# Attention by pairs of heads: the last rows of two heads in one tile, x^T of both in one accumulation, reciprocals spread by TensorE, and an order that a list scheduler makes

## The chip, the cores and the metric

The kernel runs on one core of one Trainium2 chip. Its time is device microseconds of one execution, as the median of several runs; smaller is better. A core has TensorE (PE: matmuls and the weight loads, PEld, that go with them), VectorE (DVE), ScalarE (ACT), GpSimd (POOL) and SyncE (SP), which here issues the DMAs. Each works through its own instructions in order.

## The reference

Three layers follow one another; the change touches the first alone.

```python
# q, k, v: 2 batches x 8 heads x 576 rows x 64;  f: 2 x 8 x 576
scores = scale * (q @ k.T)                      # 576 x 576 a head
cum = cumsum(log(clip(f, 1e-4, 1)))
scores = where(causal, -1e9, scores + cum[:, None] - cum[None, :])
scores -= scores.max(-1)
attn = exp(scores); attn /= attn.sum(-1) + 1e-9
x = attn @ v                                    # -> 1152 tokens x 512
# layer 2: 8 experts on all tokens, each token's expert weights found by 8 rounds of
#          normalising over experts and tokens:  out += P[:, e] * (relu(x @ w1[e]) @ w2[e])
# layer 3: the same with noisy logits, top 2 experts a token
```

All of it is float32. Matrix products are made of float32r parts: a number is split in a high part and the rest (hi, lo), and hi*hi + hi*lo + lo*hi are summed in PSUM.

## The kernel before

Attention comes first, then the gate and layer 2, then layer 3. `attention()` works head by head, 16 heads, two of them (a pair) sharing the 128 rows of x^T. A head's 576 rows are five tiles of rows t = 0..4: four of 128 rows, where tile t needs the first 128 (t + 1) columns, and a last one of 64 rows and 576 columns. The steps of a head, with their lines:

- `split_q` (L237): q is split in hi and lo, stacked as 128 columns; k is loaded twice side by side. `prep_mm` (L288) turns both by TensorE into PSUM (five transposes each), `prep_hi` (ACT) and `prep_lo` (DVE) write q1, k1 and k2 to SBUF.
- `score_mm` (L254): two matmuls a tile and one with the mask. `score_max` (L278, DVE): adds the running sum `cb`, writes P and the row's extreme. `score_exp` (L284, ACT): the exponential and the row's sum.
- `recip` and `weigh` (L319 to L332, DVE): one over the row sums, in two parts a head, and P times it, tile by tile.
- `turn_mm` (L334), `turn_hi` (ACT), `turn_lo` (DVE): P^T by transposes on TensorE, split into `pth` and `ptl`.
- `value_mm` (L360): x^T of the head. The stationary operand holds [v_hi v_lo] in its 128 columns, so that the two halves of the result's rows have to be added: `value_copy` (L374, ACT) brings one half over, `value_add` (L379, DVE) adds it. `x_parts` splits x^T into xh and xl.

PSUM has eight banks: two single ones named t, two named s, two named o, and one double one named w, through which q's and k's transposes and the scores of the last rows go.

The order is written out by hand. Each step has a time in units of a score tile (five a head): `at(g - 5 + t + D_MAX[t], score_max, n, t)`, with the tables D_* at the top; all steps are sorted by that time and issued, each to its engine. In the second batch's heads (from g = 50) the 96 matmuls of layer 2's first unit are put between them (`fill_mm`, L396, here called fills: they need xh and xl of the first batch, and expert 0's w1). SP loads q, k, v of a pair and `cb`, a row of the running sum spread over 128 partitions, two pairs ahead.

## Time and profile before

| | |
|---|---|
| three runs | 1254.22, 1255.77, 1260.47 us; median 1255.77 |
| the profiled execution | 1257.79 us, its span 1256.1 us |
| attention, first score to the first matmul behind it | 11.98 to 183.70 us |
| TensorE busy over the span | 1206.5 us (96%), mean granted clock 0.981 |
| DVE, ACT, POOL busy | 575.2, 402.8, 178.0 us |

The page cuts the span into 40 slices of 31.4 us; attention is the first six. A window's row gives the length, then each engine's busy time with its number of instructions, the TensorE clock granted (1.00 is 2.4 GHz, 0.50 is 1.2 GHz), and the DMA engines' share. Matmuls overlap in the records, so TensorE's price of something is read from start to start, not from the duration.

### The profile page before, as it was taken

The page shows a single profiled execution, that of the slowest core. Times are in us where ns is not written, and L with a number is a line of the kernel's source. Part 1 is how long each engine was busy: PE and PEld are TensorE (multiplying, and loading weights), DVE is VectorE, ACT ScalarE, POOL GpSimd, SP SyncE. Part 2 cuts the span into 40 slices and gives each one's busy share as a digit, 9 for nine tenths or more (in the row PEclk, how much of TensorE's full clock was granted, in tenths as well). Part 3 has the DMA queues.
Part 4 walks back from the last instruction along what each step waited for, and adds up shares of the span by engine and source line. Part 5 has one row for each costly group of instructions (what it writes and reads, how often), then busy time and mean ns, then how long its engine had stood idle before and what let it go on. Part 6 is the DMA issues. An engine that isn't in the chain of part 4 may idle for free. (4 is left out here: it accounts for less than half of the span.)

```text
span 1256.1 us, 17681 instructions
## 1 busy us (share of the span) xinstructions
PE 1206.5 (96%) x6965; PEld 1089.3 (87%) x6965; DVE 575.2 (46%) x1203; ACT 402.8 (32%) x796; POOL 178.0 (14%) x276
## 2 busy tenths in 40 slices
PE   7889999999999999999999999999999987999996
PEld 5667789999999999999999999999888877999995
DVE  6999876423323323223233132333455653655541
ACT  5767652212212212112122122122123443444440
POOL 4353320000000000000000000000022124343332
PEclk9988899999999999999999999999999998999998
DMA  6535113202202102012021020222021466686632
GB/s 140 133 97 125 48 52 128 68 1 67 67 2 67 39 29 68 19 49 67 1 68 38 30 68 1 67 68 67 26 93 59 135 198 178 200 224 223 180 103 62
DMA packets 112476, 105.35 MB, mean 84 GB/s; under 512 B 53102, under 2 KB 88046, under 8 KB 112383
## 3 DMA queue, kind: packets, MB, share of 16 engines
q1 hardware_dynamic: 99231, 89.86, 24.3%
q0 software_dynamic: 13152, 14.27, 4.2%
q8 instruction: 56, 0.92, 0.3%
q14 instruction: 37, 0.30, 0.1%
HBM read 94.47 MB, written 9.98 MB: 83 GB/s over the span
## 5 line engine op out<-in xcount | busy, mean ns | idle before, releaser
L131 PE MATMUL h<-xh,w1h 128*128 128x384 f32 (+8 forms) x1056 | 336.7, 319 | 2.8 <-DVE htl L516 2.3
L133 PE MATMUL h<-xh,w1l 128*128 128x384 f32 (+8 forms) x1056 | 334.2, 317 | 0.0
L132 PE MATMUL h<-xl,w1h 128*128 128x384 f32 (+8 forms) x1056 | 334.2, 316 | 0.0
L515 ACT ACTIVATE hth<-h 128x384 fp32r<-128x384 f32 (+8 forms) x264 | 119.0, 453 | 474.6 <-PE h L133 473.5
L521 PE MATMUL y<-w2h,hth 128*128 128x512 f32 (+1 forms) x624 | 244.6, 392 | 0.0
L523 PE MATMUL y<-w2h,htl 128*128 128x512 f32 (+1 forms) x624 | 243.8, 391 | 0.0
L522 PE MATMUL y<-w2l,hth 128*128 128x512 f32 (+1 forms) x624 | 243.6, 390 | 0.0
L516 DVE SCALAR_TENSOR_TENSOR htl<-h,hth 128x384 fp32r<-128x384 f32 (+8 forms) x264 | 132.8, 508 | 185.5 <-ACT hth L515 184.5
L131 PEld LDWEIGHTS h<-xh,w1h 128*128 128x128 f32 x1056 | 199.3, 189 | 5.5 <-DVE htl L516 3.3
L132 PEld LDWEIGHTS h<-xl,w1h 128*128 128x128 f32 x1056 | 199.3, 189 | 1.0
L133 PEld LDWEIGHTS h<-xh,w1l 128*128 128x128 f32 x1056 | 199.3, 189 | 0.0
L523 PEld LDWEIGHTS y<-w2h,htl 128*128 128x128 f32 (+1 forms) x624 | 116.9, 187 | 25.2 <-DVE htl L949 0.2
L522 PEld LDWEIGHTS y<-w2l,hth 128*128 128x128 f32 (+1 forms) x624 | 117.1, 188 | 23.7
L521 PEld LDWEIGHTS y<-w2h,hth 128*128 128x128 f32 (+1 forms) x624 | 117.1, 188 | 23.7
L667 DVE SCALAR_TENSOR_TENSOR acc<-y,Pgate,acc 128x512 f32<-128x512 f32 x52 | 39.0, 750 | 201.7 <-PE y L523 201.7
L849 POOL DMA_INDIRECT table_scratch<-rows,place x18 | 17.5, 975 | 786.7 <-DVE place L841 723.8
L127 DVE TENSOR_TENSOR w1l<-raw,w1h 128x1024 fp32r<-128x1024 f32 x68 | 83.1, 1223 | 75.7 <-ACT w1h L126 73.2
L126 ACT CAST w2h<-raw 128x1024 fp32r<-128x1024 f32 x68 | 70.2, 1053 | 95.6 <-PE y L523 90.8
L127 DVE TENSOR_TENSOR w2l<-raw,w2h 128x1024 fp32r<-128x1024 f32 x68 | 81.0, 1221 | 39.9 <-ACT w2h L126 37.9
L126 ACT CAST w1h<-raw 128x1024 fp32r<-128x1024 f32 x68 | 71.4, 1050 | 82.3 <-PE h L132 54.6
L969 PE MATMUL y<-htl,w2h 128*128 128x282 f32 (+5 forms) x192 | 58.3, 303 | 0.7 <-DVE htl L516 0.7
L967 PE MATMUL y<-hth,w2h 128*128 128x282 f32 (+5 forms) x192 | 58.7, 306 | 0.0
(242 smaller groups left out, 1267.4 us busy)
## 6 DMA issues: line engine op xcount, KB each, us to landing
raw<-in_moe_w_dram SPq DMA_DIRECT2D x136, 512.0 KB
cb<-ncum_scratch SPq DMA_DIRECT2D x7, 576.0 KB
raw_k<-in_k_dram SPq DMA_DIRECT2D x30, 128.0 KB
out_dram<-zer SPq DMA_DIRECT2D x1, 2304.0 KB
x_scratch<-acc SPq DMA_DIRECT2D x9, 256.0 KB
raw_q<-in_q_dram SPq DMA_DIRECT2D x16, 128.0 KB
raw_v<-in_v_dram SPq DMA_DIRECT2D x16, 128.0 KB
raw_k<-in_k_dram SPq DMA_DIRECT2D x15, 32.0 KB
```

The source lines that it names most:

```text
L126: nc.scalar.copy(hv, rv)
L127: nc.vector.tensor_tensor(lv, rv, hv.bitcast(F32), op=OP.subtract)
L131: nc.tensor.matmul(pt[:, :n], w1h[:, kc, fs], ah[:, kc, :], start=kc == 0, stop=False)
L132: nc.tensor.matmul(pt[:, :n], w1h[:, kc, fs], al[:, kc, :], start=False, stop=False)
L133: nc.tensor.matmul(pt[:, :n], w1l[:, kc, fs], ah[:, kc, :], start=False, stop=kc == KC - 1)
L515: nc.scalar.activation(hh[:, fc, :n], pt[:, :n], AF.Relu)
L516: nc.vector.scalar_tensor_tensor(hl[:, fc, :n], pt[:, :n], 0.0, hh[:, fc, :n].bitcast(F32), op0=OP.max, op1=OP.subtract)
L521: nc.tensor.matmul(py[:m], hh[:, fc, ts], w2h[:, fc, :], start=fc == 0, stop=False)
L522: nc.tensor.matmul(py[:m], hh[:, fc, ts], w2l[:, fc, :], start=False, stop=False)
L523: nc.tensor.matmul(py[:m], hl[:, fc, ts], w2h[:, fc, :], start=False, stop=fc == FC - 1)
L967: nc.tensor.matmul(py[:, :caps[l]], w2h[:, fc, dsl], ht[0][:, fc, :caps[l]], start=fc == 0, stop=False)
L969: nc.tensor.matmul(py[:, :caps[l]], w2h[:, fc, dsl], ht[1][:, fc, :caps[l]], start=False, stop=fc == FC - 1)
```

## The change

Attention is done by pairs of heads.

- The last 64 rows of both heads of a pair are one tile of 128 rows, `PL`. `last_mm` makes its scores in one accumulation: q1 of a head is kept with 64 columns of zeros beside it (`Q1`), so that head 0's product fills the first 64 rows and head 1's the last 64. Maximum, exponential, row sum and transposes of the tile are then one instruction (or five transposes) for two heads. A tile `cl` holds the running sums of both heads for it, loaded by two DMAs of 64 partitions.
- x^T of both heads goes into one accumulation in the double bank o. The stationary operand is 128 columns with v of one head in its half and zeros in the other, of v_hi in one pass and v_lo in another: three passes (hi hi, hi lo, lo hi) in place of two, and no halves to add.
- P is no longer weighed. `recip` makes the reciprocals of the nine row sums of a pair at once; `widen` (POOL) spreads them over columns, `spread_mm` (TensorE, into w) turns them so that they lie over the columns of x^T, `spread_copy` (ACT) brings them to SBUF, and `x_mul` (DVE) multiplies x^T by them on its way out of PSUM.
- q1, k1 and k2 have one buffer for each of the pair's heads. The fills use the banks s.
- The tables D_* and their times are gone. A class `Plan` gets each step with its engine, an estimated time, a place (a priority), the steps that it needs and the PSUM ring that it takes or gives back, and makes the order by list scheduling: again and again the step that could start first, by place among those that could start within 0.12 of it. `add` is called for every step.

The diff, cut:

```diff
-D_START = [-6.7, -5.65, -6.01, -5.65, -5.74, -4.38, -3.37, -4.16, -3.5]
-D_MAX = [0.82, 0.12, 1.62, 0.87, 1.52]
...
+    def order(self):
...
+                at = max([free[eng]] + [end[j] + (self.delay[tasks[j][0]] if tasks[j][0] != eng else 0.02) for j in after] +
+                         ([min(slots[ring])] if ring else []))
+                best.setdefault(eng, []).append((at, place, i))
...
+                first = min(found)[0]
+                at, place, i = min((x for x in found if x[0] <= first + 0.12), key=lambda x: (x[1], x[2]))
+                picks.append((at, place, i))
...
+            PL = [ap.tile([128, S + 64], F32, name=f"PL{i}") for i in range(2)]
...
+            def load_last(p):
+                CL[p] = ap.tile([128, S], F32, name="cl", bufs=1)
+                for h in range(2):
+                    spread_rows(CL[p][h * 64:h * 64 + 64], 2 * p + h, 64, 1, S)
...
+            def last_mm(p):
+                sp = ps.tile([128, 2, 512], F32, name="w", bufs=1)
+                for z in range(2):
+                    kk = slice(z * 288, z * 288 + 288)
+                    for h in range(2):
+                        qt = Q1[h][:, 512:640] if h == 0 else Q1[h][:, 0:128]
+                        nc.tensor.matmul(sp[:, z, :288], qt, K1[2 * p + h][:, kk], start=h == 0, stop=False)
+                        nc.tensor.matmul(sp[:, z, :288], qt, K2[2 * p + h][:, kk], start=False, stop=h == 1 and z == 0)
+                nc.tensor.matmul(sp[:, 1, 224:288], twoi, maskb[:, 0:64], start=False, stop=True)
+                two = "p (z x) -> p z x"
+                SC[p] = (sp[:, :, :288], PL[p % 2][:, 0:S].rearrange(two, z=2), CL[p].rearrange(two, z=2), 8, p)
...
+            def recip(p):
+                rs = ap.tile([128, 9], F32, name="rs", bufs=2)
+                nc.vector.tensor_scalar(rs, SUM[p % 2], 1e-9, None, op0=OP.add)
                 nc.vector.reciprocal(rs, rs)
-            def weigh(n, t):
-                m = 128 if t < 4 else 64
-                x = PP[n % 2][0:m, POFF[t]:POFF[t] + (128 * (t + 1) if t < 4 else S)]
-                nc.vector.tensor_scalar(x, x, RS[n][0:m, t:t + 1], None, op0=OP.mult)
+                RS[p] = rs
+            def widen(p):
+                rs = RS.pop(p)
+                nc.gpsimd.tensor_copy(RBX, rs[:, 0:8, None].to_broadcast([128, 8, 64]))
+                nc.gpsimd.tensor_scalar(RBL, blk, rs[:, 8:9], None, op0=OP.mult)
+            def spread_mm(p):
+                pt = ps.tile([128, 2, 512], F32, name="w", bufs=1).rearrange("p z x -> p (z x)")
+                for t in range(4):
+                    nc.tensor.transpose(pt[:, t * 128:t * 128 + 128],
+                                        RBX[:, 2 * t:2 * t + 2, :].rearrange("p h x -> p (h x)"), ident)
+                nc.tensor.matmul(pt[:, 512:576], RBL, fold, start=True, stop=True)
+                RB[p] = pt[:, 0:S]
...
+            def turn_last(p, u):
+                pt = ps.tile([128, 512], F32, name="t", bufs=2)
+                j0, j1 = ((0, 3), (3, 5))[u]
+                for j in range(j0, j1):
+                    nc.tensor.transpose(pt[:, (j - j0) * 128:(j - j0) * 128 + 128], PL[p % 2][:, j * 128:j * 128 + 128],
+                                        ident)
+                TU["l", p, u] = ([pt[:, 0:(j1 - j0) * 128].rearrange("p (j h x) -> p j h x", h=2, x=64)] +
+                                 [PX[z][1][:, j0:j1].rearrange("p j (g x) -> p j g x", x=64)[:, :, 0:6:5, :]
+                                  for z in range(2)])
...
-            def value_copy(n, u):
-                c0, w, nj = VP[u]
-                TM[n, u] = ap.tile([128, 320], F32, name="tmp", bufs=2)
-                nc.scalar.copy(TM[n, u][HALF[n % 2], :w], PO[n, u][HALF[1 - n % 2], :w])
-            def value_add(n, u):
-                c0, w, nj = VP[u]
-                mine = HALF[n % 2]
-                nc.vector.tensor_tensor(XF[n // 2][mine, c0:c0 + w], PO.pop((n, u))[mine, :w],
-                                        TM.pop((n, u))[mine, :w], op=OP.add)
...
+                if h == 0 and u == 0 and zp == 0:
+                    PO[p] = ps.tile([128, 2, 512], F32, name="o", bufs=1)
+                for zv in range(2 - zp):
+                    for j in range((2, 5)[u]):
+                        if u == 0:
+                            c0, c1 = 64, 320
+                            px = PX[zp][0][:, 1:3, :] if j == 0 else PX[zp][0][:, 0:4:3, :]
+                        else:
+                            c0, c1 = ((0, 320), (64, 384))[h]
+                            if h == 0 and j == 0 and zp == 0 and zv == 0:
+                                c1 = 384
+                            if h == 0 and j == 4:
+                                c1 = 256
+                            if h == 1 and j > 2:
+                                c0 = 128
+                            px = PX[zp][1][:, j, c0:c1]
+                        nc.tensor.matmul(PO[p][:, u, c0:c1], VS[p % 2][:, j, zv, h * 64:h * 64 + 128], px,
+                                         start=n % 2 == 0 and zp + zv + j == 0,
+                                         stop=n % 2 == 1 and zp == 1 and j == (1, 4)[u])
+            def x_mul(p):
+                o, r = PO.pop(p), RB.pop(p)
+                XF[p] = ap.tile([128, S], F32, name="xf", bufs=1)
+                two = "p (z x) -> p z x"
+                nc.vector.tensor_tensor(XF[p][:, 0:512].rearrange(two, z=2), o[:, :, 64:320],
+                                        r[:, 0:512].rearrange(two, z=2), op=OP.mult)
+                for h in range(2):
+                    rows, c0 = slice(h * 64, h * 64 + 64), h * 320
+                    nc.vector.tensor_tensor(XF[p][rows, 512:576], o[rows, 1, c0:c0 + 64], r[rows, 512:576], op=OP.mult)
...
-                    FT[fc] = ps.tile([128, 512], F32, name="o", bufs=2)
+                    FT[fc] = ps.tile([128, 512], F32, name="s", bufs=2)
...
+            plan = Plan({"PE": 0.22, "ACT": 0.1, "DVE": 0.1, "POOL": 0.12, "SP": 2.2},
+                        {"t": 2, "s": 2, "w": 1, "o": 1})
...
+                    free = done(*(("sc", n - 2, t) for t in range(4)), ("lmm", p - 1))
+                    ids["pq", n] = at("PE", 0.55, n - 0.95, done(("sq", n)) + free, prep_mm, n, "q", open="w")
+                    ids["qh", n] = at("ACT", act(576), n - 0.9, done(("pq", n)), prep_hi, n, "q", close=done(("pq", n)))
+                    ring = "o" if n < 2 else "w"
+                    ids["pk", n] = at("PE", 0.55, n - 0.85, done(("lk", p), ("tk", n)) + free, prep_mm, n, "k", open=ring)
+                    ids["kh", n] = at("ACT", act(576), n - 0.8, done(("pk", n)), prep_hi, n, "k")
+                    ids["kl", n] = at("DVE", dve(576), n - 0.75, done(("kh", n)), prep_lo, n, close=done(("pk", n)))
...
+                ids["lmm", p] = at("PE", mm(288, 8) + 0.08, b + 0.9,
+                                   done(*((x, n) for n in hp for x in ("qh", "kl")), ("ll", p), ("tlm", p - 2, 1)),
+                                   last_mm, p, open="w")
...
+                        free = done(("va", n - 1, u > 0, 1))
+                        ids["tm", n, u] = at("PE", w / 128 * 0.1, x, done(*(("se", n, t) for t in ((0, 1), (2,), (3,))[u])) + free,
+                                             turn_mm, n, u, open="t")
...
+                            ids["va", n, u, zp] = at("PE", cols / 2400 + 0.0133 * (2, 5)[u] * (2 - zp), x,
+                                                     done(*need, ("sv", p), ("va", n, 0, 0), ("va", n - 1, 1, 1)),
+                                                     value_mm, n, u, zp, open="o" if first else None)
...
+                ids["rm", p] = at("PE", 0.75, b + 2.6, done(("wi", p)), spread_mm, p, open="w")
+                ids["rc", p] = at("ACT", act(576), b + 2.7, done(("rm", p), ("xm", p - 1)), spread_copy, p, close=done(("rm", p)))
+                ids["xm", p] = at("DVE", 1.1, b + 3.3, done(("rc", p), ("va", b + 1, 1, 1), ("xp", p - 1)), x_mul, p,
+                                  close=done(("va", b, 0, 0)))
...
+                            ids["fm", fc, kc] = at("PE", mm(G, 3), x + 0.2 * kc, done(*(("xp", i) for i in range(NP)),
+                                                   ("cw", fc // 2), ("fm", fc, kc - 1)),
+                                                   fill_mm, fc, kc, open="s" if kc == 0 else None)
...
+            plan.run()
```

How the order moves, at three places; a row is one instruction, or several alike (x4), with the tiles it writes and reads. First TensorE from its first instruction to the first score, before (w and o receive the transposes of q and k of the first two heads, t the running sum; P_105 holds that sum here, s the scores):

```order
L204 MATMUL t<-P_105,ident 128x256
L304 MATMUL w<-identr,qs 128x128 x4
L304 MATMUL w<-identr,qs 128x64
L304 MATMUL o<-ident,raw_k 128x128 x4
L304 MATMUL o<-ident,raw_k 128x64
L204 MATMUL t<-P_105,ident 128x320
L304 MATMUL o<-ident,raw_k 128x128 x4
L304 MATMUL o<-ident,raw_k 128x64
L261 MATMUL s<-k_160,q_158 128x256
```

and of the change, where P_104 holds the sum and q_111 and k_215 are head 0's q1 and k1:

```order
L264 MATMUL t<-P_104,ident 128x512
L308 MATMUL o<-ident,raw_k 128x128 x4
L308 MATMUL o<-ident,raw_k 128x64
L308 MATMUL w<-identr,qs 128x128 x4
L308 MATMUL w<-identr,qs 128x64
L308 MATMUL w<-identr,qs 128x128 x4
L308 MATMUL w<-identr,qs 128x64
L329 MATMUL s<-k_215,q_111 128x256
```

The running sum is spread in one matmul ahead of all, and q of head 1 is turned ahead of the first score, k of head 1 behind it.

Then DVE where the second and the third head overlap (P_104, P_105: P of a pair's heads; L281 is the maximum of a tile with its reading of the extreme, L332 the weighing, L358 turn_lo, L382 value_add), before:

```order
L325 TENSOR_SCALAR rs<-sums_107 128x3
L326 RECIPROCAL rs<-rs 128x3
L332 TENSOR_SCALAR P_104<-P_104,rs 128x128
L332 TENSOR_SCALAR P_104<-P_104,rs 128x256
L332 TENSOR_SCALAR P_104<-P_104,rs 128x384
L281 ISA P_104,nm<-w,cb 64x576
L281 ISA nm 64x1
L358 TENSOR_TENSOR ptlb<-t,pthb 128x5x64
L382 TENSOR_TENSOR xf<-o,tmp 64x256
L281 ISA P_105,nm<-s,cb 128x128
```

and of the change, at its first reciprocals (L351 is the maximum, L417 turn_lo, L361 and L362 the reciprocals, L321 the low part of k):

```order
L417 TENSOR_TENSOR ptlb<-t,pthb 128x2x2x64
L361 TENSOR_SCALAR rs<-sums_109 128x9
L362 RECIPROCAL rs<-rs 128x9
L351 ISA P_104,nm<-s,cb 128x512
L351 ISA nm 128x1
L417 TENSOR_TENSOR ptla<-t,ptha 128x384
L321 TENSOR_TENSOR k_473<-w,k_469 128x576
L417 TENSOR_TENSOR ptlb<-t,pthb 128x3x128
L417 TENSOR_TENSOR ptlb<-t,pthb 128x4x128
```

Three weighings stood behind one part of the reciprocals; now none does, and the reciprocals serve both heads.

Last, TensorE at the end of attention, up to what follows it (L131 to L133 before and L173 to L175 now are the fills, L371 and L438 the values, L342 and L391 the transposes of P), before:

```order
L371 MATMUL o<-pthb,vs_99 128x320 x3
L371 MATMUL o<-pthb,vs_99 128x256 x2
L371 MATMUL o<-ptlb,vs_99 128x320 x3
L371 MATMUL o<-ptlb,vs_99 128x256 x2
L131 MATMUL o<-xh,w1h 128x384
L132 MATMUL o<-xl,w1h 128x384
L133 MATMUL o<-xh,w1l 128x384
L131 MATMUL o<-xh,w1h 128x384
L132 MATMUL o<-xl,w1h 128x384
L133 MATMUL o<-xh,w1l 128x384
L131 MATMUL o<-xh,w1h 128x384
L132 MATMUL o<-xl,w1h 128x384
```

and of the change, where rbx and rbl are the spread reciprocals, and L710 the gate's first matmul:

```order
L391 MATMUL t<-ident,P_105 128x128 x7
L374 MATMUL w<-ident,rbx 128x128 x4
L376 MATMUL w<-fold,rbl 128x64
L438 MATMUL o<-ptha,vs_99 128x256 x4
L438 MATMUL o<-ptla,vs_99 128x256 x2
L438 MATMUL o<-pthb,vs_99 128x320 x3
L438 MATMUL o<-pthb,vs_99 128x256 x2
L438 MATMUL o<-pthb,vs_99 128x320 x3
L438 MATMUL o<-pthb,vs_99 128x256 x2
L438 MATMUL o<-ptlb,vs_99 128x320 x3
L438 MATMUL o<-ptlb,vs_99 128x256 x2
L710 MATMUL h<-xh,wgs 16x384
```

Eight triples of fills came last before, of which three stand here; they have moved ahead of the values of the last two heads, and a value step has three passes.

## Rows read from the trace of the kernel before

**Rows 1.** The page: span, and busy tenths of DVE in 40 slices of it.
```profile
span 1256.1 us, 17681 instructions
...
DVE  6999876423323323223233132333455653655541
```

**Rows 2.** Windows, attention's two halves: length, busy us (x instructions) by engine, PEclk, DMA, GB/s.
```profile
12.00:96.00 84.00, 72.58 (x460) 55.97 (x459) 79.42 (x217) 59.12 (x154) 37.71 (x56) 0.94 0.51 127
96.00:181.00 85.00, 78.49 (x505) 66.40 (x505) 76.33 (x210) 57.64 (x145) 24.40 (x34) 0.92 0.29 71
12.00:181.00 169.00, 151.07 (x963) 122.37 (x963) 155.74 (x426) 116.75 (x298) 62.11 (x90) 0.93 0.40 99
```

**Rows 3.** Groups by line, DVE, 0 to 190 us: busy, mean ns, idle before.
```profile
L332 DVE TENSOR_SCALAR P<-P,rs 128x128 f32<-128x128 f32 (+4 forms) x80 | 42.8, 584 | 1.1
...
L382 DVE TENSOR_TENSOR xf<-o,tmp 64x256 f32<-64x256 f32 (+1 forms) x32 | 14.4, 450 | 1.7 <-ACT tmp L377 1.2
L281 DVE CUSTOM_DVE_ANT_0 P<-w,cb 64x576 f32<-64x576 f32 x16 | 11.8, 740 | 0.0
L316 DVE TENSOR_TENSOR k<-w,k 128x576 fp32r<-128x576 f32 x14 | 10.5, 751 | 2.4 <-ACT k L310 2.4
L325 DVE TENSOR_SCALAR rs<-sums 128x3 f32<-128x3 f32 (+1 forms) x32 | 8.7, 272 | 0.6 <-ACT P L286 0.6
...
L326 DVE RECIPROCAL rs<-rs 128x3 f32<-128x3 f32 (+1 forms) x32 | 5.5, 172 | 1.1
```

**Rows 4.** Timeline, PE, one head of the second half: start us, us, engine, line, tiles.
```profile
148.18 0.66 PE L342 MATMUL t<-ident,P 128*128 128x128 f32 x4
148.59 0.48 PE L261 MATMUL s<-k,q 128*128 128x512 f32 x1
...
149.79 0.34 PE L131 MATMUL o<-xh,w1h 128*128 128x384 f32 x1
...
150.31 0.40 PE L371 MATMUL o<-ptha,vs 128*128 128x256 f32 x2
150.64 0.52 PE L342 MATMUL t<-ident,P 64*128 64x64 f32 x5
151.09 0.35 PE L270 MATMUL w<-k,q 128*64 128x288 f32 x1
...
151.91 0.50 PE L371 MATMUL o<-ptla,vs 128*128 128x256 f32 x2
...
153.46 0.91 PE L371 MATMUL o<-pthb,vs 128*128 128x320 f32 x5 [0.74 <-DVE htl L404]
154.21 0.28 PE L261 MATMUL s<-k,q 128*128 128x256 f32 x1
...
158.01 0.81 PE L304 MATMUL w<-ident,raw_k 128*128 128x128 f32 x5
158.75 0.66 PE L342 MATMUL t<-ident,P 128*128 128x128 f32 x4
```

**Rows 5.** Windows of 4 us inside attention.
```profile
64.00:68.00 4.00, 1.78 (x13) 1.26 (x11) 3.96 (x7) 1.26 (x3) 2.68 (x4) 1.00 0.01 2
68.00:72.00 4.00, 4.00 (x20) 3.38 (x19) 3.93 (x12) 2.96 (x8) 3.09 (x4) 0.57 0.19 31
...
132.00:136.00 4.00, 4.00 (x19) 3.72 (x19) 3.34 (x8) 1.55 (x3) 1.86 (x4) 0.50 0.96 224
```

**Rows 6.** Timeline, all engines, before the first score.
```profile
5.90 1.19 PE L204 MATMUL t<-P,ident 16*128 16x256 f32 x2 [5.90 <-DVE P L219]
...
7.94 1.41 PE L304 MATMUL o<-ident,raw_k 128*128 128x128 f32 x5
8.04 0.65 ACT L310 ACTIVATE q<-w 128x576 fp32r<-128x576 f32 x1 [2.29 <-PE w L304]
...
11.98 0.58 PE L261 MATMUL s<-k,q 128*128 128x256 f32 x1
```

**Rows 7.** Timeline, PE, the first matmul behind attention.
```profile
183.70 0.34 PE L563 MATMUL h<-xh,wgs 128*16 128x384 f32 x1
```

More of the change, by code (lines that the diff above doesn't have):

```diff
@@ L320, in recip @@
[L320 to L332 removed]
+                h = n % 2
@@ new lines, in score_mm @@
+            def score_mm(n, t):
+                p, h = divmod(n, 2)
+                c0 = t * 128 + h * 128
+                sp = ps.tile([128, 512], F32, name="s", bufs=2)
+                w = max(256, 128 * (t + 1))
+                qt = Q1[h][:, c0:c0 + 128]
+                nc.tensor.matmul(sp[:, :w], qt, K1[n][:, :w], start=True, stop=False)
+                nc.tensor.matmul(sp[:, :w], qt, K2[n][:, :w], start=False, stop=False)
+                nc.tensor.matmul(sp[:, t * 128:t * 128 + 128], identb, maskb, start=False, stop=True)
+                SC[n, t] = (sp[:, :128 * (t + 1)], PP[h][:, POFF[t]:POFF[t + 1]], CB[p][:, h, 0:128 * (t + 1)],
+                            2 * t + h, p)
@@ L334, in turn_mm, with spread_copy @@
+            def spread_copy(p):
+                r = ap.tile([128, S], F32, name="rb", bufs=1)
+                nc.scalar.copy(r, RB[p])
+                RB[p] = r
             def turn_mm(n, u):
@@ new lines, in attention, with act, dve, pool @@
+            plan = Plan({"PE": 0.22, "ACT": 0.1, "DVE": 0.1, "POOL": 0.12, "SP": 2.2},
+                        {"t": 2, "s": 2, "w": 1, "o": 1})
+            def act(n):
+                return 0.15 + 0.00088 * n
+            def dve(n):
+                return 0.15 + 0.00104 * n
+            def pool(n, two=True):
+                return 0.12 + (0.0026 if two else 0.00098) * n
+            def mm(n, times=1):
+                return times * (n / 2400 + 0.0133)
+            at, ids = plan.add, {}
```

427 lines of the change are left out of this document (219 added, 208 removed).

## The prediction

> **What bounds the kernel now.** I read the page's forty slices first, to find the stretch that the change touches: attention is all that it edits, and attention is where DVE's tenths stand at 9 and 8, the first six slices [rows 1]. Then the windows of its two halves: in 12 to 96 us DVE is busy 79.4 of 84 us, in 96 to 181 it is busy 76.3 of 85; ACT has 59.1 and 57.6, GpSimd 37.7 and 24.4 [rows 2]. So in the first half DVE is the bound, with 5% left. In the second half two engines are near full: the matmuls of the expert layer's first unit ("fills", 96 of them) are dealt in there, so TensorE has little left too. The groups by line say what DVE spends: the weighing of P by the reciprocal sums (L332) alone takes 42.8 us [rows 3]. The timeline of TensorE gives the price of a head: from 148.18 to 158.75 is one full head, 10.57 us [rows 4]. Of that, 12 fills take 2.08 (three from 149.79 to 150.31 take 0.52) and one stop 0.74, so a head's own work with its small stops is 7.75. Attention runs from the first score at 11.98 to the first matmul behind it at 183.70: 171.7 us [rows 6, 7]. What follows is the same code, in TensorE's hands from its first row, and I carry it over unchanged: 1256.1 - 183.7 = 1072.4 us [rows 1, 7].
>
> **DVE.** Gone: the weighing, 42.8; the adding of two halves of x (L382), 14.4; half of the reciprocals and their adds (L325, L326), (8.7 + 5.5)/2 = 7.1; half of the sixteen 64-row maxima of the last rows, 11.8/2 = 5.9, since one 128-row instruction now does two heads and the number of partitions does not set the time (576 columns of k on 128 rows take 751 ns, 576 on 64 rows 740) [rows 3]. Sum 70.2. New: the product of x and the reciprocals per pair, 512 + 64 + 64 columns; 576 columns take 740, so 0.66, and two small ones which I put at 0.17 each like L326: 1.0 a pair, 8 in all. DVE's 155.7 us [rows 2] become about 94. It stops being the bound, and so does ACT, which loses two copies a head and half the last rows' exponentials and gains one copy of 576 columns (0.65, [rows 6]) a pair: below 116.8 us. GpSimd gets two small instructions a pair and keeps far from full. What is late next is TensorE.
>
> **TensorE, a head.** Added: the four products P_high v_high, P_high v_low, P_low v_high now go as three passes of narrower stationaries instead of two wide ones, 14 matmuls become 21; five of them take 0.75 (153.46 to 154.21), two of 256 columns 0.33, so seven more cost 7 x 0.14 = 1.0. The last rows' transposes: five of 64 rows cost 0.45 a head (150.64 to 151.09), five of 128 rows for two heads cost 5 x 0.10 = 0.5 (four take 0.41, 148.18 to 148.59), that is 0.25 a head: -0.2. The last rows' scores, 0.82 a head (151.09 to 151.91), become eight matmuls and one mask a pair; at a fifth of 0.82 each that is 1.5 a pair, -0.1 a head. The spreading of reciprocals: four transposes 0.41 and one small product, which the trace does not show; between 0.05 (half a 128-column transpose) and 0.6 (the 256-column fp32 one of L204 at half clock, 1.19 for two) I take 0.1, nearest to the transposes: 0.5 a pair, +0.25 [rows 4, 6]. A head: 7.75 + 1.0 - 0.2 - 0.1 + 0.25 = 8.7.
>
> **The sum.** 16 heads x 8.7 = 139.2, 96 fills x 0.173 = 16.6, less 2.0 for three of the first pair's four turnings of q and k, which lie ahead of the first score: 153.8. The start: TensorE's first rows change. The sum over the gate f is spread in one matmul of 512 columns ahead of everything (two of 256 take 1.19, so about 2.3 with its two parts, where before 1.2 stood), then k, q and already q of head 1 are turned; ACT copies q and the second half of k before it copies k of head 0. Spread until 8.3, k until 9.7, q until 10.7, ACT's q 0.65, its copies (320 columns of k, by its 0.65 for 576 at most 0.6), k 0.65, DVE's k 0.75: the first score at 13.4 instead of 11.98. The store of the running sum now stands in SP's queue before the loads of head 1's q and k; it waits for the running sum on DVE, which TensorE got at 5.90, so these loads leave some 2 us later; TensorE's wait for them falls inside the same 1.4. The first pair has nothing beside it and runs at the low clock at first (five turnings of k 1.41 here, 0.74 later: [rows 4, 6]): 3.5. Waits that the new order adds: in the first half there are no fills to put into a gap, 2.0 on top of the stops that are already inside 7.75. The end: before, eight triples of fills ran behind the last values and covered the tail; now the values of head 15 come last, then the product, xh on ACT and xl on DVE, about 0.65 + 0.35 + 0.65 + 0.75; the gate's first 8 to 14 matmuls need none of it and cover all but 0.5. Together 13.4 + 153.8 + 3.5 + 2.0 + 0.5 = 173.2, against 183.7: 10.5 us earlier. Almost all of it comes from the first half; in the second a head with its fills needs 8.7 + 2.1 = 10.8, what it takes today. The profiled execution took 1257.8 us with a span of 1256.1, 2.0 above the runs' median of 1255.8; the same 10.5 off the median gives 1245.
>
> The DMAs are hidden by prefetch: per pair one load more (the running sum for the last rows goes in two of 64 partitions, the other narrows from 576 to 512 columns). The first half's DMA share is 0.51 now [rows 2]; a pair in 17.4 us instead of 21 with 0.23 MB more on about 1.9 makes it near 0.7. If that cover went, a late load of one pair would cost a landing, about 2 us, each.
>
> **The clock.** From 64 to 68 us TensorE was busy 1.78 of 4 us, and in the next 4 us its granted clock averaged 0.57; at 132 to 136 it stood at 0.50, the level of 1.2 GHz [rows 5]. The halves' means, 0.94 and 0.92, mean some 24 us at the low level, (0.06 x 84 + 0.08 x 85) x 2, while DVE was the bound and little was lost [rows 2]. I sum at 2.4 GHz, because the gaps stood before DVE's weighing, which goes. The Trainium skill, "TensorE: Matmul & The Clock Gate", Part 1, says that "the default state is throttled, and activity releases the throttle": by it a TensorE that is denser would keep the clock, as in my sum, and one that is made to wait would pay twice. The trace agrees as far as the drop behind the gap at 64 us goes.
>
> **Rivals.** (1) The order fits well: the stops inside 7.75 shrink to nothing new (0.35 a head) and the ramp to 1 us: 16 x 0.35 + 2.5 = 8.1 more, 1237. For it: nothing but TensorE is near full, and fills stand ready in half of the stage. Against: the first half has no filler. (2) The double bank w becomes the wait: it is one buffer, and a pair passes through it six times: q twice (at most k's 0.74, and ACT 0.65), k twice (0.74, ACT 0.65, DVE 0.75), last rows (1.5 + 0.74), reciprocals (0.5 + 0.65), with hand-overs of 0.3 about 12.1 us of the 17.4. If each also queues 1 us behind other work on ACT or DVE the first half's pairs take 19 instead of 17.4 + 0.5: +5 to +8 over four pairs and the second half, 1251. For it: six uses of one buffer in a shorter pair; against: 12 us of holding leave 5 free. (3) Slower: TensorE, now the bound, waits at the hand-overs of each pair and falls to the low clock. Its place is the turn from one pair to the next, where q1, k1 and k2 have one buffer a head; its price is half of each us at 1.2 GHz. As much low clock as today, 24 us, takes 12 and leaves no gain; from 34 us on it is slower by over 0.5%; 5 us in each of eight pairs, 40 us, gives +20: 1265. For it: the drops of [rows 5]; against: what made those gaps goes. The clock rule above is what speaks for this rival. That the change does not do what it says is excluded by the order: no weighing row is left.
>
> **How the numbers follow.** A measurement here tells no change from one within 0.5%, 6.3 us. Chances: forecast (1239 to 1249) 0.50, rival 1 0.18, rival 2 0.20, rival 3 0.12. Faster: nine tenths of the forecast, rival 1, and a fifth of rival 2, 0.45 + 0.18 + 0.04 = 0.67. Slower: two thirds of rival 3 and a little of the others, 0.10. Between: 0.23. The bounds of the unknown costs are small: the small product 0.05 to 0.6 a pair, -0.4 to +4 us over the eight pairs; the added values between 0.12 and 0.17 each, -2 to +3. Eight in ten: 1233 to 1257, with the forecast's own 1239 to 1249.
>
> **What would show it.** Right: DVE busy about 60% of attention and no longer followed by TensorE's waits; first score near 13.4, first matmul behind attention near 173; pairs of the first half near 17.5 us, of the second near 21.5; granted clock above 0.95 from 25 us on. Wrong: w or t of the transposes waiting for ACT for more than a few us in sum (rival 2), granted clock below 0.9 (rival 3), pairs of the second half above 22 us, or a start later than 15 us.

## The result and the profile after

The changed kernel takes 1242.6 us (median of 4 runs, 1241.0 to 1243.3) against 1255.7 of the kernel before (4 runs beside it, 1254.2 to 1260.5): a ratio of 0.9888, with a 95% interval of 0.986 to 0.9916. The prediction was 1245, with 1233 to 1257 around it. The profiled execution took 1243.3 us.

The page answers to [rows 1]: the span, and two rows of tenths over 40 slices.

```profile
span 1241.5 us, 17746 instructions
...
DVE  5776566331322313313323223223455653646541
...
PEclk9999999999999999999999999999999998999999
```

DVE, at 6 to 9 in the first six slices before (9, 9, 9, 8 and 7 from the second on), is at 5 to 7. Windows, the counterpart of [rows 2, 5] (length, busy us by engine, granted clock, DMA share, GB/s; attention now ends at 166 us):

```profile
12.00:96.00 84.00, 82.21 (x590) 70.91 (x591) 59.80 (x166) 61.75 (x157) 46.53 (x78) 1.00 0.70 171
96.00:166.00 70.00, 69.90 (x501) 64.43 (x500) 39.55 (x108) 39.96 (x102) 19.31 (x29) 1.00 0.21 59
...
64.00:68.00 4.00, 4.00 (x36) 3.92 (x35) 3.42 (x9) 3.30 (x9) 0.00 (x0) 1.00 0.86 193
68.00:72.00 4.00, 4.00 (x33) 3.93 (x33) 2.20 (x8) 3.10 (x9) 0.24 (x1) 1.00 0.07 16
```

TensorE is busy 82.2 of 84 us in the first half where it was 72.6, DVE 59.8 where it was 79.4, and the granted clock is 1.00, the level of 2.4 GHz, where it was 0.94 and 0.92. The groups by line of DVE, 0 to 170 us, against [rows 3]:

```profile
L351 DVE CUSTOM_DVE_ANT_0 P<-s,cb 128x128 f32<-128x128 f32 (+1 forms) x64 | 30.8, 485 | 17.7 <-PE s L331 17.2
L417 DVE TENSOR_TENSOR ptlb<-t,pthb 128x384 fp32r<-128x384 f32 (+2 forms) x48 | 27.0, 569 | 13.7 <-ACT pthb L413 13.5
...
L446 DVE TENSOR_TENSOR xf<-o,rb 128x512 f32<-128x512 f32 x8 | 5.5, 689 | 4.4 <-PE o L438 3.7 <-POOL qs L286 0.7
...
L450 DVE TENSOR_TENSOR xf<-o,rb 64x64 f32<-64x64 f32 x16 | 3.5, 217 | 0.1
```

The line of weighing, 42.8 us, is gone, and the lines of the pair's product (L446, L450) take 9.0. What DVE waits for now is TensorE's scores and ScalarE's copies. The start of TensorE, with ScalarE's two rows on which its first score hangs, answers to [rows 6]:

```profile
5.39 2.04 PE L264 MATMUL t<-P,ident 16*128 16x512 f32 x2 [5.39 <-POOL blk L499]
7.36 1.41 PE L308 MATMUL o<-ident,raw_k 128*128 128x128 f32 x5
8.70 0.99 PE L308 MATMUL w<-identr,qs 128*128 128x128 f32 x5
...
9.73 0.65 ACT L314 ACTIVATE q<-w 128x576 fp32r<-128x576 f32 x1 [1.27 <-PE w L308]
10.71 0.64 ACT L317 ACTIVATE k<-o 128x576 fp32r<-128x576 f32 x1
...
11.41 0.58 PE L329 MATMUL s<-k,q 128*128 128x256 f32 x1
12.20 0.58 PE L330 MATMUL s<-k,q 128*128 128x256 f32 x1 [0.21 <-DVE k L321]
```

The first score is at 11.41. A pair can be read off the row in which DVE multiplies x by the reciprocals; there are eight of them, and the first four are

```profile
38.62 0.69 DVE L446 TENSOR_TENSOR xf<-o,rb 128x512 f32<-128x512 f32 x1 [0.30 <-PE o L438]
55.82 0.69 DVE L446 TENSOR_TENSOR xf<-o,rb 128x512 f32<-128x512 f32 x1 [0.31 <-POOL qs L286]
72.79 0.68 DVE L446 TENSOR_TENSOR xf<-o,rb 128x512 f32<-128x512 f32 x1
90.05 0.69 DVE L446 TENSOR_TENSOR xf<-o,rb 128x512 f32<-128x512 f32 x1 [0.37 <-POOL qs L286]
```

so a pair takes 17.2, 17.0 and 17.3 us; the later ones stand at 111.79, 132.48, 153.27 and 166.27, which is 21.7, 20.7 and 20.8 a pair with the fills, and 13.0 for the last. The end, against [rows 7], in TensorE's timeline:

```profile
165.29 0.84 PE L438 MATMUL o<-ptlb,vs 128*128 128x320 f32 x5
165.97 0.34 PE L710 MATMUL h<-xh,wgs 128*16 128x384 f32 x1
```

The gate's first matmul comes at 165.97 instead of 183.70, 17.7 us earlier, and directly behind the last values. From there to the end the span has 1241.5 - 165.97 = 1075.5 us, 3.1 more than the 1072.4 of before.

### The profile page after: what moved, and what is told of

Same layout as the page of the kernel before. It is cut to its first block, busy times and chain, and to the rows that moved or that the text cites. A ratio compares the mean times of both kernels' runs of the same rounds, so it can differ in the third digit from the quotient of the medians.

```text
span 1241.5 us, 17746 instructions
## 1 busy us (share of the span) xinstructions
PE 1205.1 (97%) x7075; PEld 1098.7 (88%) x7075; DVE 518.0 (42%) x1048; ACT 387.4 (31%) x753; POOL 182.7 (15%) x300
## 5 line engine op out<-in xcount | busy, mean ns | idle before, releaser
L173 PE MATMUL h<-xh,w1h 128*128 128x384 f32 (+8 forms) x1056 | 336.6, 319 | 3.0 <-DVE htl L663 2.4
L175 PE MATMUL h<-xh,w1l 128*128 128x384 f32 (+8 forms) x1056 | 334.2, 316 | 0.0
L173 PEld LDWEIGHTS h<-xh,w1h 128*128 128x128 f32 x1056 | 199.2, 189 | 5.7 <-DVE htl L663 3.5
L175 PEld LDWEIGHTS h<-xh,w1l 128*128 128x128 f32 x1056 | 199.3, 189 | 0.0
```

The lines of the kernel that those rows point to most:

```text
L173: nc.tensor.matmul(pt[:, :n], w1h[:, kc, fs], ah[:, kc, :], start=kc == 0, stop=False)
L175: nc.tensor.matmul(pt[:, :n], w1l[:, kc, fs], ah[:, kc, :], start=False, stop=kc == KC - 1)
```

## The experiments

Two marks serve throughout: a pair's pitch (the time between two such rows of x) and the time of the gate's first matmul, "the gate": 183.7 before, 166.0 after. Four groups of runs had their own runs of the kernel before beside them (medians 1255.8, 1259.7, 1256.2 and 1257.3), so across groups the ratios are compared.

**a_before_no_weigh.** What is the weighing alone worth?

```
-                for t in range(5):
-                    at(g + D_WEIGH[t], weigh, n, t)
```

> The kernel before without its 80 weighings of P on DVE (the division by the row sums is left out; the sums and reciprocals are still made). Theory (DVE bounds the first half of attention, TensorE the second): DVE loses 42.8 us, a head of the first half falls from 10.5 to 7.75 to 8.5 us, the half from 84 to 64 to 68, the second half gains 4 to 6 at most: 1230 to 1236 us in all. Rival (the hand-written order and its hand-overs set the pace, not DVE's busy time): a gain below 8 us, 1248 or more.

Measured: 1226.4 us, ratio 0.9756 (0.9724 to 0.9788). One window and the gate:

```profile
12.00:96.00 84.00, 82.01 (x585) 66.50 (x584) 75.69 (x225) 75.22 (x194) 43.96 (x68) 1.00 0.64 160
...
153.03 0.34 PE L561 MATMUL h<-xh,wgs 128*16 128x384 f32 x1
```

The time lies below the theory's range. TensorE goes from 72.6 to 82.0 busy, its clock from 0.94 to 1.00, and a pair takes 15.1 to 16.2 in the first half, though DVE is still busy 75.7 of 84 us there. The gate comes 30.7 us earlier, against 17.7 with the whole change: what takes DVE's weighing away gives more than the whole gain, and the rest of the change gives part of it back.

**b_after_weigh.** The changed kernel with 72 multiplications of the weighing's size, by a column of ones, planned between the exponential and the turn:

```
+ nc.vector.tensor_scalar(x, x, onec, None, op0=OP.mult)
+ ids["we", n, t] = at("DVE", dve(w), x + 0.25, done(("se", n, t)), weigh, n, t)
```

> The changed kernel with a weighing of every P tile put back on DVE (times a column of ones, planned with the rest): 72 instructions, about 40 us. Theory (DVE's relief made the gain): DVE's 113 us of the first 180 become about 153, pairs of the first half go from 17.1 to 19 to 20.5 us, the second half's hardly: 1251 to 1257 us. Rival (the list-made order made the gain): pairs stay at 17.1 to 17.6, 1246 or less.

Measured: 1257.5 us, ratio 1.0015 (0.9997 to 1.0033), just past the theory's 1251 to 1257. The whole gain is gone. A window of this run, a row of GpSimd, TensorE's two longest waits from 12 to 96 us, and the gate:

```profile
12.00:96.00 84.00, 73.11 (x476) 61.48 (x477) 62.54 (x166) 52.36 (x131) 39.79 (x66) 0.94 0.65 161
...
37.80 0.21 POOL L192 CAST wgs<-wg 128x32 fp32r<-128x32 f32 x1 [7.38 <-DMA wg<-in_moe_w_gate_dram]
...
PE w L381 <- POOL rbx L375: 3.8, 1, 3.8
PE s L329 <- DVE nm L351: 3.3, 2, 2.2
...
183.40 0.34 PE L719 MATMUL h<-xh,wgs 128*16 128x384 f32 x1
```

But the planner made another order for it, and not all of the loss is DVE's. The first pair's reciprocals are ready at 33.9 us, but in GpSimd's queue the split of the gate's weights stands ahead of their widening and waits 7.38 us for its load. TensorE stops 3.8 us for the first spread, its clock averages 0.57 in the 4 us from 40 on, and the first row of x comes at 46.5 instead of 38.6: 7.9 of the 17.4 us that are lost at the gate. The next three pairs take 24.0, 18.5 and 16.1 us, a mean of 19.5 as the theory had it, with DVE busy only 62.5 of 84 us. The weighing also stands in the chain from exponential to turn. So the run agrees that DVE's relief made the gain, but it doesn't divide the weighing from the fault in GpSimd's queue, nor DVE's sum from the chain.

**c_after_two_of_three.** The changed kernel without the third value pass (the low half of P):

```
+                if zp == 1:
+                    return
```

> The changed kernel without the third value pass, P_low times v_high, which is left out of the result: 7 matmuls of 0.146 us a head less, 16.4 us of TensorE. Theory (TensorE bounds all of attention after the change): all of it comes off, 8 in each half, 1226 to 1229 us. Rival (the double bank w or the hand-overs set the first half's 17.1 us a pair): only the second half shrinks, 1233 to 1236 us.

Measured: 1233.7 us, ratio 0.9806 (0.9767 to 0.9844), the gate at 158.6. The rival was right: the second half takes 18.4 to 20.4 a pair in place of 20.7 to 21.7, the first 17.3 to 17.7, no less than with the pass. TensorE's waits from 36 to 89 us (sum, times, longest), first of the changed kernel, then of this one:

```profile
PE w L308 <- DVE nm L351: 0.9, 1, 0.9
PE s L330 <- DVE k L321: 0.5, 2, 0.3
```

```profile
PE w L308 <- DVE nm L351: 3.5, 3, 1.3
PE s L330 <- DVE k L321: 1.1, 3, 0.4
PE t L405 <- DVE ptlb L417: 0.6, 1, 0.6
PE s L329 <- ACT k L317: 0.5, 2, 0.3
```

```profile
158.57 0.34 PE L712 MATMUL h<-xh,wgs 128*16 128x384 f32 x1
```

What the shorter passes free turns into waits, above all for the one buffer w, which the last rows hold until DVE has taken their maximum. In the first half, relieving TensorE alone makes no pair shorter: the fourth row of x comes only 1.1 us earlier.

**f_two_pass.** The same saving in a complete version: stationaries [v_high v_low] as before the change, the halves added by ScalarE and DVE. The reciprocals, too, go another way than in the change: their spread is placed behind the pair's last values, isn't copied by ScalarE, and holds w until DVE has multiplied x out of it. Cut:

```
- for zv in range(2 - zp):
-     nc.tensor.matmul(PO[p][:, u, c0:c1], VS[p % 2][:, j, zv, h * 64:h * 64 + 128], px, ...
+ nc.tensor.matmul(o, VS[p % 2][:, j, h, :], px, start=zp == 0 and j == 0, stop=zp == 1 and j == (1, 4)[u])
```

> The changed kernel with the values as before: two passes with v_high and v_low in one stationary, the halves added by ACT (copy) and DVE (add), and the reciprocals applied to the sum in SBUF straight from PSUM. TensorE has 16.4 us less, ACT 12.6 more and 5 less, DVE 14.4 more. Theory (TensorE is the bound, ACT and DVE have room): 6 to 13 us off, 1230 to 1237. Rival (ACT and DVE, near 15 us a pair each, or the hand-overs through o take it back): 1240 or more.

Measured: 1236.9 us, ratio 0.9841 (0.9809 to 0.9872), the gate at 160.6; the pairs at 17.1, 17.2 and 19.1 in the first half and 18.9 to 19.9 in the second. The median is below both kernels', though the interval touches the changed kernel's (0.986 to 0.9916). What it gains on the changed kernel again comes only behind the first half.

**g_old_order.** The order and the tiles of the kernel before, with only the weighing replaced:

```
- at(g + D_WEIGH[t], weigh, n, t)
+ at(g + D_RECIP[1] + 0.05, widen, n)
+ at(g + (8.4 if last else 11.8), spread_mm, p)
+ at(g + 5 + D_X - 0.05, x_mul, p)
```

> The kernel before, with its order written out by hand, its own tiles for the last rows of each head and its two value passes with copied halves; only the weighing is replaced: the reciprocals of both heads are widened by GpSimd, turned by TensorE into w (five transposes a pair), copied by ScalarE and multiplied onto x^T in one VectorE operation a pair. Theory (the gain is the 72 weighings leaving VectorE; the joint tile, the joint accumulation and the planned order are not needed for it): the kernel before without weighing took 1226.4; TensorE is busy all the time there in the first half (51.0 of 52 us), so five transposes add about 0.7 us a pair, 8 x 0.7 = 5.6: 1232 (1228 to 1236). Rival (the sixth use of the single double bank w holds the turns of q and k, as where the change is run without its low value pass: 1.3 us of TensorE's wait a pair): 8 x (0.7 + 1.3) = 16: 1242 (1238 to 1246).

Measured: 1238.8 us beside 1259.7, ratio 0.9835 (0.9819 to 0.9852), the gate at 165.4. By the ratio that is 1235 at 1255.7, inside the theory's 1228 to 1236. But its price was too low: a pair takes 17.0 to 18.1 in the first half, 1.9 to 2.4 more than in a, of which the theory counted 0.7. From 36 to 90 us TensorE waits 1.9 us in three times for DVE's low half of k, before the last rows' scores, and 1.9 us in two for the low half of P, before the turns; the turns of q and k, which the rival named, don't wait. What matters is the level:

```profile
165.41 0.34 PE L585 MATMUL h<-xh,wgs 128*16 128x384 f32 x1
```

With the reciprocals on x, the old tiles and the old order reach the gate 0.6 us before the change does. The joint tile, the joint accumulation and the planned order together bring nothing beside them. That isn't said of each: f, with planned order and joint tile but the old two passes, has its gate 4.8 us before g's, at nearly the same ratio.

**h_c_no_spread.** Run c, and also no spreading of the reciprocals (x is copied):

```
-                pt = ps.tile([128, 2, 512], F32, name="w", bufs=1)...
-                for t in range(4): nc.tensor.transpose(...)
+                return
```

> The changed kernel without the low value pass (as in c_after_two_of_three) and also without widening, spreading and copying the reciprocals: x^T is copied, not divided. The plan and its order stay the same; w has five uses a pair in place of six. In the first half of c TensorE was busy 45.9 of 52 us and a pair still took 17.3 to 17.7. Theory W (the uses of w, one after the other, set the pace of the first half): a pair takes 16.0 to 16.6 there, the time is 1225 to 1229. Rival (w is held by what stands in VectorE's order ahead of the maximum of the last rows, and by other hand-overs that stay; the spread only fills a gap): a pair takes 17.0 to 17.6, the time is 1230 to 1234.

Measured: 1229.0 us, ratio 0.9762 (0.9738 to 0.9785), at 1255.7 this is 1226, in theory W's range; but the pairs take 16.1, 17.1 and 16.8, between the two, and the gate is at 153.7, 4.9 before c:

```profile
153.70 0.34 PE L702 MATMUL h<-xh,wgs 128*16 128x384 f32 x1
```

That is 0.6 us a pair on average, what the spread itself takes on TensorE (162.56 to 163.14 in the changed kernel's timeline), but 3.9 of the 4.9 are there by the fourth row of x (85.1 instead of 88.9). The wait of w for the maximum stays, 2.8 us, as the rival said. So one use of w less helps the first half more than the second and doesn't free it; since GpSimd's widening and ScalarE's copy go with it, the run doesn't show that it is w.

**d_fills_last.** The changed kernel with the fills behind the last values:

```
- if p == NP - 1:
+ if p == NPT - 1:   (and every fill waits for ("va", NH - 1, 1, 1))
```

> The changed kernel with one edit: the 96 fill matmuls of the first expert wait for the last values, so the second half of attention runs without them and they come after it. Theory (TensorE has no room beside attention, in either half, so a fill costs its full time wherever it stands): the second half runs at the first half's pitch of 17.1 us a pair, the last multiplication of x at about 38.6 + 6 x 17.1 + 13 = 154, and the fills add their 16 to 17 us behind it: gate's first matmul 165 to 168, the time 1242 to 1245. Rival (the fills use gaps that attention leaves in the second half, so part of them is free there): gate's first matmul 170 or later, the time 1247 to 1252.

Measured: 1240.4 us, ratio 0.9849 (0.9832 to 0.9867). DVE's product rows of the second half and the gate:

```profile
106.18 0.69 DVE L446 TENSOR_TENSOR xf<-o,rb 128x512 f32<-128x512 f32 x1 [0.37 <-POOL qs L286]
122.59 0.69 DVE L446 TENSOR_TENSOR xf<-o,rb 128x512 f32<-128x512 f32 x1 [0.37 <-PE o L438]
138.40 0.69 DVE L446 TENSOR_TENSOR xf<-o,rb 128x512 f32<-128x512 f32 x1 [0.37 <-PE o L438]
...
165.62 0.34 PE L710 MATMUL h<-xh,wgs 128*16 128x384 f32 x1
```

The gate hardly moves, 165.6 for 166.0: a fill costs its full time wherever it stands. But a pair without fills takes 16.5, 16.4 and 15.8 us here, less than the theory's 17.1 and the 17.2 of the first half. The first half has work of its own: four pieces of the first expert's w1 are split by ScalarE and DVE (1.04 and 1.22 us each). The ratio is below the changed kernel's, with intervals that touch, and 1237 at 1255.7 is below the theory's 1242 to 1245, though the gate is where it was; the time behind the gate was 1073.0 in this profile, on which more below.

**j_conv_pool** and **k_after_conv_pool** give these pieces to GpSimd, in f and in the changed kernel:

```
- at("ACT", 2.2, 5.0 + 2 * c, done(("lw", c)), conv_w, 0, 0, (c,))
+ at("POOL", 4.5, 5.0 + 2 * c, done(("lw", c)), conv_w, 0, 0, (c,), True)
```

> The two-pass version f_two_pass (1236.9) with one more edit: the first expert's w1, four pieces of 1024 columns that are split during attention, is split by GpSimd alone in place of ScalarE and VectorE. It takes 4 x 1.05 us from ScalarE and 4 x 1.22 from VectorE in the first half. Theory (in the trace of c the maximum of the last rows stands behind such a piece on VectorE, and TensorE waits 1.3 us a pair for it): the first half loses 0.6 to 1.3 us in each of four pairs: 1232 to 1234.5. Rival (GpSimd's long operations stretch VectorE's beside them, as the weighings of the kernel before were stretched from 285 to 1687 ns, or the wait moves to the next hand-over): 1236 to 1240.

> The changed kernel with one edit: the four pieces of the first expert's w1 are split by GpSimd alone, not by ScalarE and VectorE. With the fills put last (d_fills_last) a pair of the second half took 15.8 to 16.5 us, against 17.1 of the first half, where these pieces are split and the work on TensorE is otherwise the same. Theory (the pieces cost the first half 0.7 us a pair through ScalarE and VectorE, and TensorE, shown busy 16.9 of 17 us there, isn't at its peak): a pair of the first half takes 16.3 to 16.6, gate's first matmul is at 163 to 164, the time 1239 to 1241 on a chip that gives the changed kernel 1242.6. Rival (TensorE is the bound in the first half): a pair stays at 17.0 to 17.3, gate's first matmul at 165.5 to 166.5, the time within 1 us of the changed kernel's. A third way: GpSimd's queue makes the split of q late, and a pair takes more than 17.3.

j took 1233.9 us beside 1259.7, ratio 0.9797 (0.9781 to 0.9814). That is 1230 at 1255.7, beside which f has its 1236.9: a larger gain than the theory forecast (1232 to 1234.5). It is the fastest version with all of the work in it, though its interval touches f's. Its profiled execution was 4.7 us above its median, so its pairs, 17.1 to 19.9, and its gate at 162.2, later than f's, don't show where the time came from; the theory's mechanism isn't shown. k took 1244.3, ratio 0.9896 (0.9871 to 0.9922), no gain. Its rows of x, and below them two windows and a wait of TensorE:

```profile
59.47 0.69 DVE L446 TENSOR_TENSOR xf<-o,rb 128x512 f32<-128x512 f32 x1 [0.37 <-PE o L438]
75.95 0.69 DVE L446 TENSOR_TENSOR xf<-o,rb 128x512 f32<-128x512 f32 x1 [0.37 <-POOL qs L286]
92.36 0.69 DVE L446 TENSOR_TENSOR xf<-o,rb 128x512 f32<-128x512 f32 x1 [0.37 <-POOL qs L286]
```

```profile
32.00:36.00 4.00, 1.53 (x9) 1.36 (x10) 0.40 (x1) 0.35 (x1) 3.91 (x5) 0.91 0.90 203
36.00:40.00 4.00, 4.00 (x24) 3.83 (x24) 0.98 (x4) 1.76 (x6) 3.84 (x5) 0.67 0.84 151
...
PE w L374 <- POOL rbx L368: 3.5, 1, 3.5
```

With the row before them (42.73) the pairs take 16.7, 16.5 and 16.4 in place of 17.1, the theory's pace. But the first piece stands in GpSimd's queue ahead of the first pair's widening, waits there 4.26 us for its own load, and TensorE stops 3.5 us for the spread; the clock then falls to 0.67 for the next window. The first row of x comes at 42.73 instead of 38.62, and 2.3 us of loss are left at the gate (168.3).

**m_copy_rb.** j with the spread reciprocals copied out of w at once by ScalarE, and the spread no longer placed behind the pair's last values:

```
+ nc.scalar.copy(r, RB[p])
- ids["rm", p] = at("PE", 0.55, b + 3.0, done(("wi", p), ("va", b + 1, 1, 1)), spread_mm, p, open="w")
+ ids["rm", p] = at("PE", 0.75, b + 2.6, done(("wi", p)), spread_mm, p, open="w")
```

> The version j_conv_pool with the spread reciprocals copied out of w by ScalarE at once, as in the changed kernel, in place of being held in w until the multiplication of x. In j TensorE waited 1.9 us in three pairs for that multiplication to leave w. Theory (the hold of w is what is late): 0.6 us a pair less in the first half: 3 to 5 us below j, a ratio to the kernel before of 0.976 to 0.978 against j's 0.980. Rival (ScalarE, busy 70% there, passes the wait on, or the next use of w is late by another hand-over): no more than 1 us from j, 0.979 to 0.982.

Measured: 1242.8 us, ratio 0.9883 (0.9849 to 0.9917): neither, worse than j. The edit also puts the spread earlier, as in the changed kernel, and with that m got k's fault, TensorE waiting 3.2 us for the first widening; its pairs took 17.2 to 20.2. So the run says nothing on the hold of w.

**n_old_conv_pool.** The pieces to GpSimd in g, whose order is written out:

```
- at(24.9 + 10 * c + D_CONV, conv_w, 0, 0, (c,))
+ at(24.9 + 10 * c + D_CONV, conv_w, 0, 0, (c,), True)
```

> The version g_old_order (the order of the kernel before, reciprocals onto x) with the first expert's four pieces split by GpSimd alone, as in j_conv_pool. In g a pair takes 17.0 us before the first piece (58.6 us) and 18.1 behind it, with ScalarE and VectorE busy 85% there; the order is written out, so no piece stands ahead of the widening that TensorE waits for, as it did in k_after_conv_pool. Theory (the pieces cost a pair 0.8 to 1.1 us through ScalarE and VectorE): three to four pairs at 17.0 to 17.4 and 3 to 4 us less in all, a ratio to the kernel before of 0.980 to 0.9815 against g's 0.9835. Rival (a pair is held there by the turns and the weight loads, not by the pieces): pairs at 18.0, 0.983 to 0.985.

Measured: 1237.5 us, ratio 0.9848 (0.9832 to 0.9864). The pairs are the theory's: 17.0, 17.0, 17.0 and 17.5 for 17.0, 18.1, 18.1 and 18.6, and the gate is at 161.7 for 165.4. But the ratio isn't below g's 0.9835: the two intervals overlap by most of their width, so the 3.7 us at the gate are not shown in the time.

**after_again.** The changed kernel a second time, with no edit, for what lies behind the gate:

> The changed kernel once more, with another profile, beside the two runs above. In the first profile the span from gate's first matmul to the end was 1075.5 us, 3.1 more than in the kernel before, all of it in the gathers of the last layer; the code there is the same, and the other runs so far show 1071.0 to 1074.1. Theory (it belongs to the run and not to the kernel): gate's first matmul at 165.5 to 166.5 again, and 1071 to 1074.5 behind it. Rival (the earlier start makes the gathers collide with the loads of weights every time): 1075 to 1076 again.

Measured: 1242.6 us, ratio 0.988 (0.9851 to 0.9909), the gate at 165.45, and 1242.4 - 165.45 = 1077.0 us behind it: beyond even the rival's 1075 to 1076, so the loss came again.

## Why the prediction was right, point by point

**The total** was right and its parts were not: 7.2 us more came from attention (the gate at 166.0, predicted 173.2) and 3.1 were lost behind it, which together make 14.6 for the 10.5 forecast. The medians show 13.1. That the loss behind the gate hid part of the error in attention is luck. The attention ended nearly where rival 1 put it, 173.2 - 8.1 = 165.1, but not by rival 1's ramp of 1 us, as the clock below shows.

**DVE stops being the bound: right.** Predicted about 94 us busy; the windows have 59.8 + 39.6 = 99.4. Run a shows the cause: take away the weighing alone and the gate comes 30.7 us earlier. Run g shows that the weighing's going is enough for the whole gain, with the division moved to x. Run b agrees, but a fault of its order is in its loss too. How the weighing held TensorE up can be read in the kernel before, in the last section.

**The start, 13.4, was mis-sized**, by 2.0. The spread of the sum began 0.5 us sooner and took 2.04 for 2.3, ScalarE's rows from q to k took 1.7 (9.73 to 11.41) for 1.9, and the step added DVE's 0.75 for k, for which only the second product of the first score waits (12.20, not 11.41).

**The head on TensorE, 8.7, and the waits, 2.0, were mis-sized together,** by 4.7: what the start's 2.0 and the end's 0.5 (the gate stands directly behind the last values) leave of the 7.2. With the fills, the first turnings and the ramp as forecast, 16 heads with their waits took 136.5 us instead of 139.2 + 2.0, about 8.5 a head. No run divides this further. In d a pair without fills and pieces takes 15.8 to 16.5, with TensorE busy in all of 96 to 138 us: 7.9 to 8.2 a head. In the first half, where the pieces are split, a head takes 8.5 to 8.6. So by d the head was counted too long and the waits too short, and the two errors partly cancelled, which is luck. The base of 7.75 held: in a, with the old work, a pair takes 15.1 to 16.2, which is 7.55 to 8.1 a head. The 0.95 that the steps add is near the mark too: pair for pair, the first half's 17.2, 17.0 and 17.3 are 0.6 to 1.1 a head above a's 15.1, 15.7 and 15.7.

**TensorE is late next: half right.** It is full in the first half. But without the third value pass (c) a pair of the second half got 1.6 us shorter and one of the first half no shorter, as w's wait came up in its place; and k took 0.6 a pair off the first half without touching TensorE's work, so its busy time of 82.2 in 84 was not its peak. The Trainium skill, "Perfetto Trace Analysis", Identifying the Most-Contended Engine, says that the busy share of matmuls is not a good measure of how near TensorE is to its limit, because pipelined instructions look smaller in the trace than they are; the pairs of 17.2 and 16.4 at full busy time agree.

**Rival 2, the double bank w,** was not late in the changed kernel (0.9 us in 53), but it is the next to be late: 3.5 us in c, 2.8 in h. **Rival 3** didn't come: the granted clock is 1.00 in both windows of attention. Only the start runs slower: products of 288 columns start 0.24 us apart from 17.28 to 18.48, and the next pair's, from 33.00 on, 0.13. By these rows TensorE is at the lower level for some 7 us from the first score on, though the window shows 1.00, and half of that, 3.5 us, is what the sum had for it. Rival 3's mechanism is real, as k's window at 0.67 behind a stop of 3.5 us shows, but the new order has no stop of that length.

**The second half, 21.5 a pair: right** (21.7, 20.7, 20.8), and d shows why: fills cost their full time. "Almost all from the first half" was too much: the last sum of halves of the fourth pair stood at 101.45 before and the fourth row of x stands at 90.05, 11.4 us earlier; the eighth (180.18 and 166.27) is 13.9 earlier, and 3.8 more come at the tail, where the gate no longer waits behind the last fills.

**"What follows is unchanged": off by 3 to 4.6 us,** and not settled. The code is the same, the first 780 us behind the gate agree, and the difference lies in the last layer, where TensorE waits for gathered rows (14.1 us in the changed kernel, 15.6 in its second profile, 12.4 before): 1.7 and 3.2 of the 3.1 and 4.6. In the eleven other profiles the time behind the gate is 1071.0 (a) to 1079.1 (m), and it is 1073.0 in d and 1072.9 in g, whose gates are at the changed kernel's time, so an earlier start alone doesn't bring it. What does, no run here tells.

**What the change as a whole is worth.** Without the weighing the old order reaches a gate of 153.0. Putting the division back on x costs it 12.4 us (g); the changed kernel, with its joint tile and planned order, stands 13.0 behind it. Of these, the third value pass is 7.4 (c) and the spread with its widening and copy 4.9 (h). With both gone the changed kernel's gate is at 153.7, so its tile and order bring nothing over the old ones there. The gain is that of a moved multiplication, and 13 of the 30.7 us that its going frees are paid again.

## What to carry to other kernels

When a change does several things at once, price the one that frees the bound engine by itself: here leaving the weighing out told more than any sum over the rest. Behind a removed bound two or more limits may stand close together (here TensorE, one buffer, work on the copying engines), and relieving one of them alone may then show little, as c did in the first half. An operation moved to an idle engine brings its waits along: a piece that waits 4 us for its load holds up whatever the planner put behind it in that queue, as in k and m, and so do the gate's weights in b.

## What the runs showed of the hardware

A split of 1024 columns on DVE, both of whose inputs lie in SBUF, takes 1.22 us in the changed kernel each time. In c the four pieces take 1.23, 2.25, 2.26 and 1.73, the three longer ones beside GpSimd's two operations of 640 columns, its split of v; the rows of the third, GpSimd's and then DVE's:

```profile
67.62 0.72 POOL L272 CAST vs<-raw_v 128x640 fp32r<-128x640 f32 x1 [5.03 <-DMA raw_k<-in_k_dram]
68.43 1.57 POOL L273 TENSOR_TENSOR vs<-raw_v,vs 128x640 fp32r<-128x640 f32 x1
...
68.82 2.26 DVE L169 TENSOR_TENSOR w1l<-raw,w1h 128x1024 fp32r<-128x1024 f32 x1 [0.78 <-ACT w1h L168]
```

The weighings show the same in the kernel before. Three of them in a row (128, 256 and 384 columns) beside the split of v, and, further down, the same three with no row of GpSimd's beside them, each with the wait of TensorE that follows:

```profile
44.79 2.91 DVE L332 TENSOR_SCALAR P<-P,rs 128x128 f32<-128x128 f32 x3
45.04 0.71 POOL L235 CAST vs<-raw_v 128x640 fp32r<-128x640 f32 x1
45.83 1.66 POOL L236 TENSOR_TENSOR vs<-raw_v,vs 128x640 fp32r<-128x640 f32 x1
48.52 0.68 PE L304 MATMUL w<-identr,qs 128*128 128x128 f32 x5 [1.93 <-DVE nm L281]
...
55.19 0.88 DVE L332 TENSOR_SCALAR P<-P,rs 128x128 f32<-128x128 f32 x3
56.88 0.69 PE L304 MATMUL w<-identr,qs 128*128 128x128 f32 x5 [0.17 <-DVE nm L281]
```

They take 2.91 us instead of 0.88. The maximum of the last rows stands behind them in DVE's order, and TensorE waits 1.93 us for w instead of 0.17. The same stands at 64.15, ahead of the drop of the clock in [rows 5]. So the weighing that left DVE was dearer than its columns, and part of what it cost was its meeting with GpSimd; whether moving the split of v alone would have given some of the gain, no run tests. The Trainium skill, "GPSIMD Engine Reference", 1. Specifications, names DVE's contention with GpSimd for operations with two SBUF inputs or in a mode that uses both ports; the slow pieces in c, with two inputs in SBUF, agree with it.
